# A one-core fp32 attention and MLP kernel: SyncE's order fixed from the first MoE on, probability copies and head loads emitted later

## The chip, the cores and the metric

The kernel runs on one core of a Trainium2 chip. The metric is device time in microseconds (us) of one execution. TensorE (PE) does the matmuls; ScalarE (ACT), VectorE (DVE) and GpSimd (POOL) do the rest of the arithmetic; SyncE (SP) issues nearly all DMA transfers. Each engine works through its own instructions in a fixed order and stands still when the next one has to wait.

## What is computed

```python
def _attn_ref(q, k, v, g_q, g_k):           # q, k, v: (4, 12, 448, 64)
    q_n, k_n = rmsnorm(q, g_q), rmsnorm(k, g_k)
    scores = np.matmul(q_n, k_n.transpose(0, 1, 3, 2)) / np.sqrt(64)
    attn = np.exp(scores - scores.max(-1, keepdims=True))
    attn = attn / (attn.sum(-1, keepdims=True) + 1e-09)
    return np.matmul(attn, v)
# x: attention's output as (1792, 768)
def _moe_ref(x, w_in, w_out):               # 768 -> 2048 -> 768
    r = np.maximum(x @ w_in, 0.0)
    return (r * r) @ w_out
def _moe2_ref(x, w1, w2, w3, w_out):        # 768 -> 1024 -> 1024 -> 768
    return ((x @ w1) * (x @ w2) @ w3) @ w_out
```

The weights of both MLPs come as 64-bit floats, q, k and v as 32-bit ones.

## The kernel before

**Products.** Each fp32 operand is held as a high part and a low part, and each product is three matmuls (high by high, high by low, low by high; `mm3`, lines 411 to 413). In the trace they follow each other at 0.20 us. A unit of weights (128 rows by 384 or 512 columns) feeds nine or twelve matmuls of 448 columns.

**Order of the work.** One loop runs over the 48 heads (B x H, in batch order) and a 49th turn. In a turn, `stage_qk` emits the score matmuls `sc`, `stage_exp` the exponentials into `p`, `stage_t` the transposes of the probabilities of the head before (`pt`, copied to `ptr` and `pte`), `stage_v` their product with v (`kv`), and head norms and transposes of k (`kv` too, copied to `kt`) for later heads. Each head has two halves, s = 0 and s = 1. In between, `fill(n)` emits a stretch of about n matmuls of another generator, six stretches a head; a unit costs 9 or 12 of them. Heads 0 to 11 are filled with `gen_w3o` (w3 by w_out, stored in DRAM as `w3o`, so that the second MLP ends in one product), heads 12 to 23 with `gen_moe(0)`, the MLPs of the first batch, here called the **first MoE**: 16 units of w_in, 12 of w_out, again 16 and 12, then 32 of w1 and w2 and 12 of `w3o`, 100 units in all. Heads 24 to 47 are filled with batches 1 and 2 (the second MoE), and the last batch follows the loop.

**A unit's way.** In the first MoE a 64-bit unit is loaded (line 319, four buffers `raw64`), turned into 32-bit words (ACT line 333, then the low words on ACT line 337 or POOL line 339), joined (DVE line 346, into one of seven buffers `raw`), stored back to DRAM as 32-bit floats for the later batches (line 354, `f_in` and the like), and split into `hl`, the high part on ACT and the low part on POOL or DVE (lines 144 and 150). `advance(u)` emits these ahead of the matmuls of unit u: the low parts up to u + 2 (u + 4 from w1 and w2 on), high parts one further, joins two, words three, loads five further.

**Probabilities.** From head 12 on the probabilities pass through a copy from SBUF to SBUF, `pw` (line 997), which gives them the type that the transposes then read. It is emitted right behind the exponentials that it copies. For odd heads, behind s = 1, four small stores `rsd` (line 1008) send the sums of the exponentials out, and `stage_rows` reads them back as `rsw` in the next turn.

**What sets the order on an engine.** A scheduler orders the instructions of each engine by its own model of the times. `in_order(SP)` marks a point from which `chain()` ties each SyncE instruction to the one emitted before it, so that SyncE issues in emitted order from there on. Before, that point stands at head 24, behind the first MoE. `late` (line 1143) decides whether a turn's loads of the next heads (`load_head`, `load_v`, `load_group`) are emitted at the turn's start or behind its first `stage_exp`; before, it holds from head 25 on.

Of the kernel before, what the change touches and what calls it, by code (L numbers as in the profile page):

```python
# [8 lines left out]
F32 = mybir.dt.float32  # L9
F32R = mybir.dt.float32r  # L10
# [20 lines left out]
def attention_moe_kernel(  # L31
# [15 lines left out]
    nc = tc.nc  # L47
    SP, ACT, DVE, POOL, PE = (e.engine for e in (nc.sync, nc.scalar, nc.vector, nc.gpsimd, nc.tensor))
    B, P, H, C, D = k_nat.shape
    S = P * C  # L50
    QC = q_nat.shape[3]
    MIX = S - 3 * 128
    CHUNKS = (((0, 1), (2, 3)), ((4, 5), (6,)))
    NH = B * H
# [69 lines left out]
    def in_order(*engines):  # L124

        spans.append((nc.cur_bb.bb.instructions[-1], engines))
# [664 lines left out]
    def load_group(g):  # L791
        if not (0 <= g < NH // GH):
            return
        b, h0 = divmod(g * GH, H)
        qk = t1.tile([128, GH * C, D], F32, name="qn", tag="qn")
        qn = qk[:, :GH // 2 * QC]
        kn = t2.tile([P, GH, C, D], F32, name="kn", tag="kn")
        if g == 0:
            nc.sync.dma_start(out=kn[:, 0:2], in_=k_nat[0, :, 0:2])
            load_head(0)  # L800
            nc.sync.dma_start(out=qn[:, :QC], in_=q_nat[0, :, 0])
            load_to(0)
            nc.sync.dma_start(out=kn[:, 2:], in_=k_nat[0, :, 2:GH])
            nc.sync.dma_start(out=qn[:, QC:], in_=q_nat[0, :, 1])
            load_to(1)
        else:
            nc.sync.dma_start(out=kn, in_=k_nat[b, :, h0:h0 + GH])
            nc.sync.dma_start(
                out=qn, in_=q_nat[b, :, h0 // 2:(h0 + GH) // 2].rearrange("p j c d -> p (j c) d")
            )  # L810
        grp[g] = [qk, kn, None, None]
# [161 lines left out]
    def stage_exp(h, s):  # L973
        if not (0 <= h < NH):
            return
        d = heads[h]
        nb, o = d.pop("nb"), d.pop("sc")
        i = h % 2
        if s == 0 and i == 0:
            sums2[h // 2] = small.tile([128, QC], F32, name="sm", tag="sm")  # L980
        sm = sums2[h // 2]
        chunks = CHUNKS[h % 2][s]
        n = len(chunks)
        pp = t3.tile([128, 2, S], F32, name="p", tag="p")
        for j, c in enumerate(chunks):
            p = d["p"][c] = pp[:, j, :]
            if h >= H:
                nc.scalar.activation(
                    out=nb[:, j:j + 1], in_=nb[:, j:j + 1], func=AF.Copy, scale=d["rq"][:, c:c + 1]
                )  # L990
            nc.scalar.activation(  # L991
                out=p, in_=o[j], func=AF.Exp, scale=d["rq"][:, c:c + 1], bias=nb[:, j:j + 1],
                accum_out=sm[:, c:c + 1],
            )
        if h >= H:
            words = t3.tile([128, 2, S], F32R, name="pw", tag="pw")
            nc.sync.dma_start(out=words[:, :n].bitcast(F32), in_=pp[:, :n])
            for j, c in enumerate(chunks):
                d["p"][c] = words[:, j, :]
        if s == 1 and i == 1:  # L1000
            nc.scalar.activation(out=sm, in_=sm, func=AF.Copy, bias=1e-9)
            rs = rss[h // 2 % 2]
            nc.vector.reciprocal(out=rs[:, :QC], in_=sm)
            turned = t2.tile([128, 32], F32, name="rt", tag="rt")
            nc.vector.transpose(out=turned, in_=rs)
            flat = dram.tile([QC, 128], F32, name="rsd", tag="rsd", bufs=2)
            for b in range(0, 128, 32):
                nc.sync.dma_start(out=flat[:, b:b + 32], in_=turned[b:b + QC])
            sums2[h // 2] = flat

    def stage_rows(h):
        if 0 <= h < NH and h % 2:
            flat = sums2[h // 2]
            rows = sums2[h // 2] = t1.tile([128, S], F32, name="rsw", tag="rsw")
            flat = flat.rearrange("c p -> (c p)")
            for r, to, at, n in ((0, 0, 0, S), (D, S - MIX, S, MIX), (D, 0, S + MIX, S - MIX)):
                nc.sync.dma_start(out=rows[r:r + D, to:to + n], in_=flat[at:at + n].partition_broadcast(D))
# [82 lines left out]
    def start_fill(gen, total):  # L1100
        state.update(gen=gen, credit=0.0, left=total)

    def fill(n):
        state["credit"] += n
        while state["gen"] is not None and state["credit"] > 0:
            try:
                k = next(state["gen"])
                state["credit"] -= k
                state["left"] -= k
            except StopIteration:  # L1110
                state["gen"] = None
# [28 lines left out]
    first.close()  # L1140
    for h in range(NH + 1):
        n = W3O / ((H + 1) * 6) if h <= H else (MOE / (H * 6) if h <= 2 * H else (MOE + IN) / (2 * H * 6))
        late = h > 2 * H
        if not late:
            load_head(h + 3)
            load_v(h + 1)
            if h % GH == 0:
                load_group(h // GH + 1)
        stage_qk(h, 0)
        fill(n)  # L1150
        stage_exp(h, 0)
        if h == 0:
            group_prep(0, "rest")
        if late:
            load_head(h + 3)
            load_v(h + 1)
            if h % GH == GH - 1:
                load_group((h + 1) // GH + 1)
        if h % H != 1:
            stage_x(h - 2)  # L1160
        stage_t(h - 1, 0)
        stage_t(h - 1, 1)
        early = H <= h and h % 2 == 0
        fill(n)
        if early:
            stage_k(h + 1)
        stage_lo(h - 1)
        if h < NH:
            v_prep(h)
        fill(n)  # L1170
        stage_rows(h - 1)
        even = H <= h
        if even:
            stage_qk(h, 1)
        if not early:
            stage_k(h + 1)
        stage_t(h - 1, 2)
        stage_t(h - 1, 3)
        fill(n)
        stage_lo(h - 1)  # L1180
        if not even:
            stage_qk(h, 1)
            fill(n)
        stage_exp(h, 1)
        fill(n)
        if even:
            fill(n)
        stage_v(h - 1)
        if h >= 2 * H and h % GH < 2:
            group_prep(h // GH + 1, "qk"[h % GH])  # L1190
        elif h % GH == 1:
            group_prep(h // GH + 1)
        head_prep(h + 2)
        if h and h % H == 0:
            if h != 3 * H:
                fill(1e9)
            stage_x(h - 1)
            if h == H:
                start_fill(gen_moe(0), MOE)
            elif h == 2 * H:  # L1200
                in_order(SP)
                start_fill(gen_late(), MOE + IN)
            elif h == NH:
                start_fill(gen_pair(), MOE)
# [61 lines left out]
```

## Time and profile before

| | |
|---|---|
| runs before | 6176.91, 1163.66 and 1156.78 us, median 1163.66 |
| profiled execution | 1160.01 us, of which the span 1158.2 us |
| mean granted TensorE clock | 0.989 of full speed |
| PE busy | 1124.9 us, 97% of the span |
| DVE busy | 796.4 us, 69% |
| ACT busy | 777.0 us, 67% |
| POOL busy | 605.2 us, 52% |

The profiled execution stands 3.65 us below the median of the runs and 3.23 us above the fastest. The span runs from the first to the last instruction. An engine is busy while one of its instructions runs; on PE, matmuls overlap, and what is not busy is time in which nothing ran there. Waits name the engine that waited, the line of the instruction that waited, and what it waited for. The first MoE takes the stretch from 180 to 450 us.

### The profile page before, as it was taken

To read this page: it belongs to the slowest core of one execution; us is meant where nothing else is said; L and a number is where in the kernel's file an instruction comes from. 1 tells how busy PE (TensorE), PEld (TensorE's weight loads), DVE (VectorE), ACT (ScalarE), POOL (GpSimd) and SP (SyncE) were. 2 spreads that over 40 slices of the span, in tenths; PEclk is the share of its full clock that TensorE was granted. 3 is DMA by queue.
4 is the path that set the end of the run, shared out by engine and by line. 5 is a ranking of instruction groups with operands and counts; after the bars stand their busy time and mean duration, and the time that the engine had idled before them with its cause. 6 is when DMAs were issued, how large, how long until landed. Compare 5 with 4: busy or idle time off the path is not lost. (4 is left out here: it accounts for less than half of the span.)

```text
span 1158.2 us, 18787 instructions
## 1 busy us (share of the span) xinstructions
PE 1124.9 (97%) x5958; PEld 1020.3 (88%) x5958; DVE 796.4 (69%) x1363; ACT 777.0 (67%) x1768; POOL 605.2 (52%) x609
## 2 busy tenths in 40 slices
PE   7889999999999999999999999999999999999998
PEld 4678888988889889989989999999999899999997
DVE  6899888978988754664675755674534315887786
ACT  6889978878978666776766676776754445533352
POOL 3375533544434355956875776684865854021131
PEclk9799999999999999999999999999999999999999
DMA  8767757888888864565655657564546764243423
GB/s 245 255 204 214 234 156 253 300 279 285 298 292 267 282 201 159 166 199 170 224 186 162 203 173 256 177 211 152 188 158 197 223 195 128 68 134 106 128 84 123
DMA packets 130899, 229.74 MB, mean 198 GB/s; under 512 B 17472, under 2 KB 84544, under 8 KB 130800
## 3 DMA queue, kind: packets, MB, share of 16 engines
q1 hardware_dynamic: 129072, 225.79, 61.5%
q10 hardware_dynamic: 1728, 2.75, 0.7%
q8 instruction: 47, 0.77, 0.3%
q14 instruction: 52, 0.43, 0.1%
HBM read 162.53 MB, written 37.05 MB: 172 GB/s over the span
## 5 line engine op out<-in xcount | busy, mean ns | idle before, releaser
L150 POOL TENSOR_TENSOR hl<-raw,hl 128x384 fp32r<-128x384 f32 (+1 forms) x286 | 332.5, 1169 | 286.4 <-ACT hl L144 249.1
L144 ACT ACTIVATE hl<-raw 128x384 fp32r<-128x384 f32 (+1 forms) x405 | 227.3, 567 | 148.9 <-PE mm L413 42.5
L411 PE MATMUL mm<-x,hl 128*128 128x448 f32 (+1 forms) x640 | 238.8, 373 | 1.3 <-ACT x L144 1.3
L412 PE MATMUL mm<-x,hl 128*128 128x448 f32 (+1 forms) x640 | 234.1, 366 | 0.7 <-DVE x L150 0.6
L413 PE MATMUL mm<-x,hl 128*128 128x448 f32 (+1 forms) x640 | 233.7, 365 | 0.0
L411 PE MATMUL mm<-act,hl 128*128 128x448 f32 (+1 forms) x544 | 201.5, 370 | 1.6 <-ACT act L144 1.6
L412 PE MATMUL mm<-act,hl 128*128 128x448 f32 (+1 forms) x544 | 198.6, 365 | 3.1 <-DVE act L150 2.5
L413 PE MATMUL mm<-act,hl 128*128 128x448 f32 (+1 forms) x544 | 197.5, 363 | 0.1
L967 DVE TENSOR_REDUCE nb<-sc 128x1 f32<-128x448 f32 x168 | 102.5, 615 | 69.8 <-PE sc L957 68.6
L411 PEld LDWEIGHTS mm<-x,hl 128*128 128x128 f32 x640 | 121.2, 189 | 11.0 <-ACT x L144 2.6
L412 PEld LDWEIGHTS mm<-x,hl 128*128 128x128 f32 x640 | 121.2, 189 | 10.2 <-DVE x L150 1.6
L413 PEld LDWEIGHTS mm<-x,hl 128*128 128x128 f32 x640 | 121.2, 189 | 9.4
L991 ACT ACTIVATE p<-sc,nb,rr 128x448 f32<-128x448 f32 x168 | 121.5, 725 | 9.6 <-DVE nb L969 6.7
L150 DVE TENSOR_TENSOR ptr<-pt,ptr 128x512 fp32r<-128x512 f32 (+1 forms) x144 | 85.9, 616 | 51.7 <-ACT ptr L144 51.3
L412 PEld LDWEIGHTS mm<-act,hl 128*128 128x128 f32 x544 | 102.5, 188 | 12.2 <-DVE act L150 4.2
L411 PEld LDWEIGHTS mm<-act,hl 128*128 128x128 f32 x544 | 102.7, 189 | 9.3 <-ACT act L144 2.3
L413 PEld LDWEIGHTS mm<-act,hl 128*128 128x128 f32 x544 | 102.6, 189 | 7.9 <-DVE hl L150 0.4
L339 POOL TENSOR_SCALAR raw<-raw 128x384 uint32<-128x384 uint16 (+1 forms) x80 | 54.2, 678 | 95.9 <-DMA raw<-w_out 19.5
L346 DVE SCALAR_TENSOR_TENSOR raw<-raw 128x384 uint32<-128x384 uint32 (+1 forms) x120 | 87.7, 740 | 21.2 <-POOL raw L339 9.4
L333 ACT ACTIVATE raw<-raw 128x384 f32<-128x384 f32 (+1 forms) x120 | 71.6, 603 | 32.9 <-DMA raw<-w 14.5
L956 PE MATMUL sc<-kt,qh 128*128 128x448 f32 (+1 forms) x192 | 75.0, 391 | 14.1 <-ACT kt L144 8.1
L150 DVE TENSOR_TENSOR hl<-raw,hl 128x384 fp32r<-128x384 f32 (+1 forms) x119 | 81.5, 687 | 8.1 <-ACT hl L144 7.9
(153 smaller groups left out, 2127.9 us busy)
## 6 DMA issues: line engine op xcount, KB each, us to landing
pw<-p SPq DMA_DIRECT2D x54, 448.0 KB
raw<-f_in SPq DMA_DIRECT2D x96, 192.0 KB
raw<-f_out SPq DMA_DIRECT2D x72, 256.0 KB
raw<-w_in SPq DMA_DIRECT2D x32, 384.0 KB
raw<-w_out SPq DMA_DIRECT2D x24, 512.0 KB
raw<-w SPq DMA_DIRECT2D x32, 384.0 KB
qt<-q_t SPq DMA_DIRECT2D x48, 224.0 KB
raw<-f SPq DMA_DIRECT2D x56, 192.0 KB
```

The lines of the kernel that those rows point to most:

```text
L144: return nc.scalar.activation(out=out, in_=in_, func=AF.Copy)
L150: return (nc.vector if eng == "v" else nc.gpsimd).tensor_tensor(out=out, in0=in0, in1=in1, op=op)
L333: nc.scalar.activation(out=hi, in_=hi, func=AF.Prelu, scale=2.0**-112, alpha=-(2.0**32))
L339: nc.gpsimd.tensor_scalar(out=t[:, :n, 0], in0=low, scalar1=2.0**-13, scalar2=2.0**-14 - 0.5, op0=ALU.mult, op1=ALU.add)
L346: nc.vector.scalar_tensor_tensor(out=f[:, :n].bitcast(U32), in0=t[:, :n, 1], scalar=3, in1=t[:, :n, 0], op0=ALU.logical_shift_left, op1=AL ...
L411: nc.tensor.matmul(ps, w[:, 0, wk, :], x[0], start=(i == 0), stop=False)
L412: nc.tensor.matmul(ps, w[:, 0, wk, :], x[1], start=False, stop=False)
L413: nc.tensor.matmul(ps, w[:, 1, wk, :], x[0], start=False, stop=(i == last))
L956: nc.tensor.matmul(out, d["qh"][:, at:at + m], d["kt"], start=True, stop=False)
L967: nc.vector.tensor_reduce(out=nb[:, j:j + 1], in_=o[j], axis=AX.X, op=ALU.max, negate=True)
L991: nc.scalar.activation(out=p, in_=o[j], func=AF.Exp, scale=d["rq"][:, c:c + 1], bias=nb[:, j:j + 1], accum_out=sm[:, c:c + 1],)
```

## The change

Three things change, all in what SyncE issues and when.

1. `in_order(SP)` moves from head 24 to head 12: it stands behind the last `fill(1e9)` of `gen_w3o` and ahead of `start_fill(gen_moe(0))`.
2. The copy `pw` leaves `stage_exp` for a function of its own, `stage_words`. For heads 12 to 24 the copy of s = 0 is emitted two stretches behind its exponentials, and that of s = 1 one or two stretches behind. From head 25 on both are emitted directly behind `stage_exp`; for odd heads that puts the copy of s = 1 behind the four `rsd` stores, where it stood ahead of them.
3. `late` holds from head 13 on: the loads of q, k and v for later heads are emitted behind the turn's first `stage_exp`. `load_group` stays where it was for heads up to 24.

```diff
         if h >= H:
-            words = t3.tile([128, 2, S], F32R, name="pw", tag="pw")
-            nc.sync.dma_start(out=words[:, :n].bitcast(F32), in_=pp[:, :n])
-            for j, c in enumerate(chunks):
-                d["p"][c] = words[:, j, :]
+            d["pp"] = pp
...
+    def stage_words(h, s):
+        if not (H <= h < NH):
+            return
+        d = heads[h]
+        chunks = CHUNKS[h % 2][s]
+        n = len(chunks)
+        words = t3.tile([128, 2, S], F32R, name="pw", tag="pw")
+        nc.sync.dma_start(out=words[:, :n].bitcast(F32), in_=d.pop("pp")[:, :n])
+        for j, c in enumerate(chunks):
+            d["p"][c] = words[:, j, :]
...
-        late = h > 2 * H
+        late = h > H
         if not late:
             load_head(h + 3)
             load_v(h + 1)
-            if h % GH == 0:
-                load_group(h // GH + 1)
+        if h <= 2 * H and h % GH == 0:
+            load_group(h // GH + 1)
         stage_qk(h, 0)
         fill(n)
         stage_exp(h, 0)
+        if h > 2 * H:
+            stage_words(h, 0)
...
             load_head(h + 3)
             load_v(h + 1)
-            if h % GH == GH - 1:
+            if h > 2 * H and h % GH == GH - 1:
                 load_group((h + 1) // GH + 1)
...
         fill(n)
+        if h <= 2 * H:
+            stage_words(h, 0)
         stage_rows(h - 1)
...
         stage_exp(h, 1)
+        if h > 2 * H:
+            stage_words(h, 1)
         fill(n)
         if even:
             fill(n)
+        if h <= 2 * H:
+            stage_words(h, 1)
         stage_v(h - 1)
...
             if h == H:
+                in_order(SP)
                 start_fill(gen_moe(0), MOE)
             elif h == 2 * H:
-                in_order(SP)
                 start_fill(gen_late(), MOE + IN)
```

The first place is SyncE's queue where `gen_w3o` ends. Before, these rows stand there; `raw64` from `w_in` are loads of the first MoE's units, `w3o` from `osb` the last stores of `gen_w3o`, and `pw` the copies for head 12.

```order
L826 DMA v_2342<-v_in 128x256
L997 DMA pw_2227<-p_2222 128x896
L439 DMA w3o_99<-osb_2239 128x3x128
L1017 DMA rsw_2267<-rsd_2169 64x448
L1017 DMA rsw_2267<-rsd_2169 64x64
L1017 DMA rsw_2267<-rsd_2169 64x384
L808 DMA qn_4367<-q_nat 128x896
L997 DMA pw_2302<-p_2297 128x896
L439 DMA w3o_99<-osb_2313 128x3x128
L818 DMA qt_2340<-q_t 128x448
L319 DMA raw64_2577<-w_in 128x768
L354 DMA f_in_114<-raw_2540 128x384
```

After the change, these stand at the same last stores.

```order
L1005 DMA rsd_2169<-rt_2167 7x32 x4
L439 DMA w3o_99<-osb_2237 128x3x128
L1025 DMA rsw_2267<-rsd_2169 64x448
L1015 DMA pw_2265<-p_2222 128x896
L1025 DMA rsw_2267<-rsd_2169 64x64
L1025 DMA rsw_2267<-rsd_2169 64x384
L1015 DMA pw_2314<-p_2297 128x896
L439 DMA w3o_99<-osb_2311 128x3x128
L319 DMA raw64_2351<-w_in 128x768
L354 DMA f_in_114<-raw_2155 128x384
L319 DMA raw64_2361<-w_in 128x768
L354 DMA f_in_114<-raw_2356 128x384
```

Of the first MoE's loads from `w_in`, 15 stand ahead of the last `w3o` store before and seven after; `raw64_2351` is the eighth, and the ninth follows right behind it.

The second place is ACT's queue among the units of w1 and w2 of the first MoE, ahead of a copy `kt` that the score matmuls of the next head read. The names in it: line 333 makes the words of a unit, `hl` is the high part of one, `p` are exponentials, `ptr` copies of transposes. Before:

```order
L144 ACTIVATE act_4961<-mm_4874 128x448
L144 ACTIVATE ptr_4710<-pt_4992 128x384
L144 ACTIVATE ptr_4717<-pt_4997 128x384
L144 ACTIVATE hl_5009<-raw_4970 128x384
L333 ACTIVATE raw64_4965<-raw64_4965 128x384
L144 ACTIVATE r_5021<-mm_4964 128x448
L337 ACTIVATE raw64_4965<-raw64_4965 128x384
L144 ACTIVATE hl_5031<-raw_5007 128x384
L333 ACTIVATE raw64_5002<-raw64_5002 128x384
L144 ACTIVATE kt_5045<-kv_5040 128x448
```

After the change, the same copy (now `kt_5043`) stands behind these.

```order
L144 ACTIVATE act_4957<-mm_4872 128x448
L333 ACTIVATE raw64_4720<-raw64_4720 128x384
L144 ACTIVATE vt_4919<-kv_4910 64x448
L144 ACTIVATE vhl_5047<-v_4697 128x4x64
L144 ACTIVATE hl_4858<-raw_4823 128x384
L333 ACTIVATE raw64_4747<-raw64_4747 128x384
L337 ACTIVATE raw64_4747<-raw64_4747 128x384
L144 ACTIVATE r_5019<-mm_4960 128x448
L144 ACTIVATE hl_4880<-raw_4856 128x384
L333 ACTIVATE raw64_4766<-raw64_4766 128x384
L144 ACTIVATE kt_5043<-kv_5038 128x448
```

The `ptr` copies are gone from there, and the words just ahead of the copy belong to older units: before it was the unit of `raw64_5002`, after it is that of `raw64_4766`, which is `raw64_4768` before, six units earlier in the program.

The third place is ACT's queue in the same part of the program, where the high part of one unit (`hl_4775` before, `hl_4773` after) is made for the first matmuls of a product of w1 and w2. Before:

```order
L144 ACTIVATE ptr_4710<-pt_4705 128x512
L144 ACTIVATE ptr_4717<-pt_4712 128x512
L337 ACTIVATE raw64_4654<-raw64_4654 128x384
L144 ACTIVATE hl_4729<-raw_4683 128x384
L333 ACTIVATE raw64_4678<-raw64_4678 128x384
L144 ACTIVATE r_4741<-mm_4677 128x448
L144 ACTIVATE hl_4756<-raw_4727 128x384
L333 ACTIVATE raw64_4722<-raw64_4722 128x384
L144 ACTIVATE hl_4775<-raw_4754 128x384
L333 ACTIVATE raw64_4749<-raw64_4749 128x384
```

After the change:

```order
L144 ACTIVATE hl_4754<-raw_4725 128x384
L991 ACTIVATE p_4981,sm_4980<-sc_4945,nb_4944,rr_3774 128x448
L144 ACTIVATE ptr_4708<-pt_4703 128x512
L144 ACTIVATE ptr_4715<-pt_4710 128x512
L333 ACTIVATE raw64_4650<-raw64_4650 128x384
L337 ACTIVATE raw64_4650<-raw64_4650 128x384
L991 ACTIVATE p_4981,sm_4980<-sc_4949,nb_4944,rr_3774 128x448
L333 ACTIVATE raw64_4674<-raw64_4674 128x384
L144 ACTIVATE hl_4773<-raw_4752 128x384
```

Before, six instructions stand between the two `ptr` copies and that high part, and no exponential is among them. After, five do, one of them an exponential (`p_4981`, of the next head), and the words among them are of units four and five earlier. What else moved is the transposes that the two copies read: in PE's order, 81 rows stand between the last of them and the first matmul of that high part before, and 18 after.

## Rows read from the trace of the kernel before

**Rows 1.** Windows by stage: PE, PEld, DVE, ACT, POOL busy us, clock, DMA share, GB/s
```profile
0.00:180.00 180.00, 161.23 (x865) 136.40 (x866) 155.36 (x315) 148.83 (x340) 83.99 (x108) 0.94 0.71 217
180.00:450.00 270.00, 261.64 (x1396) 237.90 (x1395) 217.35 (x368) 210.08 (x494) 125.38 (x134) 0.99 0.81 269
350.00:415.00 65.00, 62.61 (x332) 56.84 (x331) 52.43 (x91) 50.40 (x122) 28.24 (x31) 0.97 0.82 269
450.00:1158.00 708.00, 702.05 (x3701) 646.01 (x3699) 423.73 (x681) 418.07 (x934) 395.87 (x367) 1.00 0.53 167
```
**Rows 2.** PE's largest wait, 180 to 450: us, times, longest
```profile
PE sc L956 <- ACT kt L144: 5.7, 4, 2.4
```
**Rows 3.** SyncE's largest wait, 180 to 450
```profile
SPq L997 <- ACT ptr L144: 34.0, 8, 5.6
```
**Rows 4.** ACT's largest wait, 350 to 415
```profile
ACT raw L333 <- DMA raw<-w: 9.5, 6, 3.5
```
**Rows 5.** SyncE's timeline: start, duration, line, transfer
```profile
370.19 0.54 SPq L319 DMA_DIRECT2D raw<-w  x1
373.22 1.30 SPq L1008 DMA_DIRECT2D rsd<-rt  x4
...
375.00 0.38 SPq L319 DMA_DIRECT2D raw<-w  x1
...
381.52 0.47 SPq L997 DMA_DIRECT2D pw<-p  x1
```
**Rows 6.** ACT's timeline, same stretch; in brackets the wait ahead
```profile
378.46 0.57 ACT L333 ACTIVATE raw<-raw 128x384 f32<-128x384 f32 x1 [2.54 <-DMA raw<-w]
...
381.30 0.19 ACT L991 ACTIVATION_READ_ACCUMULATOR p<-sc,nb,rr 128x1 f32 x1
...
384.69 0.57 ACT L333 ACTIVATE raw<-raw 128x384 f32<-128x384 f32 x1
385.13 0.55 ACT L144 ACTIVATE kt<-kv 128x448 fp32r<-128x448 f32 x1
```
**Rows 7.** PE's timeline behind the longest wait
```profile
385.74 0.47 PE L956 MATMUL sc<-kt,qh 128*128 128x448 f32 x1 [2.39 <-ACT kt L144]
...
388.57 0.57 PE L413 MATMUL mm<-x,hl 128*128 128x448 f32 x1
388.95 0.57 PE L411 MATMUL mm<-x,hl 128*128 128x448 f32 x1
...
390.06 0.37 PE L412 MATMUL mm<-x,hl 128*128 128x448 f32 x1
390.26 0.37 PE L413 MATMUL mm<-x,hl 128*128 128x448 f32 x1
```
**Rows 8.** Windows with PE idle and a changing clock, columns as in group 1
```profile
30.00:60.00 30.00, 24.96 (x104) 19.74 (x103) 26.81 (x50) 26.19 (x56) 10.51 (x13) 0.81 0.82 269
90.00:120.00 30.00, 28.03 (x166) 24.94 (x165) 29.69 (x55) 27.77 (x62) 18.57 (x23) 1.00 0.78 231
...
386.00:390.00 4.00, 4.00 (x17) 3.37 (x17) 2.55 (x6) 1.08 (x3) 2.18 (x3) 0.57 1.04 327
```
**Rows 9.** Durations of ACT's and POOL's operations, 350 to 415: busy us, mean ns
```profile
L144 ACT ACTIVATE hl<-raw 128x384 fp32r<-128x384 f32 x22 | 11.5, 530 | 0.0
L991 ACT ACTIVATE p<-sc,nb,rr 128x448 f32<-128x448 f32 x10 | 7.2, 720 | 0.1
```
```profile
L150 POOL TENSOR_TENSOR hl<-raw,hl 128x384 fp32r<-128x384 f32 x11 | 12.7, 1155 | 21.2 <-ACT hl L144 20.9
```
**Rows 10.** SyncE's timeline: the last store of w3o
```profile
179.50 0.54 SPq L439 DMA_DIRECT2D w3o<-osb  x1
```
**Rows 11.** SyncE at an odd head of the second MoE; PE reading that copy
```profile
500.50 0.47 SPq L997 DMA_DIRECT2D pw<-p  x1
502.49 1.86 SPq L1008 DMA_DIRECT2D rsd<-rt  x4
```
```profile
508.80 0.63 PE L1030 MATMUL pt<-ident_r,pw 128*128 128x128 f32 x6
```

## Prediction

> **What bounds the kernel now.** I read the windows by stage first. In the profiled execution (1160.0 us, span 1158.2) PE is busy for 261.64 of the 270 us of the first MoE, where nearly all of the change lies, and for 702.05 of the 708 behind it [rows 1]. TensorE paces both, and the change neither adds nor removes a matmul. So what it can win there is what PE stands idle, 8.4 us, and what a lower clock costs. The clock of that stage is 0.99, and the low part of it sits in one place: in the 4 us from 386 to 390 it was granted at 0.57, between the two levels of 1.2 and 2.4 GHz, right behind PE's longest wait, and matmuls there start 0.38 us apart where they otherwise follow at 0.20 [rows 7, 8]. That cost 4 x (1 - 0.57) = 1.7 us. All in all 8.4 + 1.7 = 10.1 us, 0.9% of the time, is the most that an ideal order of this stage would give.
>
> Then PE's waits: of the 8.4 us, 5.7 are four waits of the scores for the copy `kt` on ACT, the longest 2.39 [rows 2, 7]. For the longest I followed the chain back. The `kt` copy starts on ACT at 385.13 and ACT has no gap ahead of it back to 378.46, where it stood 2.54 us for a unit's words [rows 6]. That unit was loaded by SyncE at 375.00, behind the stores `rsd` at 373.22, for which SyncE had stood since it issued the load before, at 370.19 [rows 5]: a transfer on its way for 3.5 us, asked for too late. SyncE stands for 34.0 us of the 270 at line 997 alone, the copies `pw`, because they are in its queue ahead of their exponentials' end [rows 3]: that of 381.52 was issued 0.03 us behind the exponentials' last instruction (381.30 + 0.19) [rows 5, 6]. In the stretch from 350 to 415 ACT's waits for words come to 9.5 us in six [rows 4].
>
> **The change part by part.**
>
> *SyncE in emitted order, copies two stretches late (gain).* A copy emitted two stretches behind its exponentials, some 28 matmuls or 5.7 us, finds them done. So SyncE no longer stands there, and the loads keep their distance of up to four units (the buffers of `raw64`) from their joins. On ACT the words move back too: the order shows them four to eight units later, and those ahead of the `kt` of the longest wait are six units older. A unit's nine matmuls take 9 x 0.20 = 1.8 us, so the word there has 6 x 1.8 = 11 us more for a transfer that was 2.5 us late. I take the four `kt` waits from 5.7 to 1.0 us (-4.7; between nothing, if ACT is late there for another reason, and -5.7), and the slow clock behind the longest of them goes with it (-1.7; between 0 and -1.7). The other waits, 2.7 us, stay.
>
> *The same order, just in time (loss).* What ACT gains ahead of `kt` it pays at the splits. Before, words stand two to ten units ahead of their high parts and these about six units ahead of the matmuls; after, words stand next to their high parts, and these three or four units, among w1 and w2 two to four, ahead of the matmuls. At the third place that the change's section shows, a chain now runs from PE's transposes to PE's matmuls. From the end of the transposes ACT does two `ptr` copies, words, low words, an exponential, words, and the high part. ACT starts copies 0.44 us apart [rows 6], the exponential takes 0.72 + 0.19 with the reading of its sum [rows 6, 9], the high part 0.53 [rows 9]: 5 x 0.44 + 0.91 + 0.53 = 3.6 us, and some 0.3 to see the transposes done. The low part on POOL takes 1.16 [rows 9], so the unit is ready after 5.1 us. PE has, up to the first matmul that needs the low part, 18 matmuls of 0.20 us and eight small transposes of which six took 0.63 [rows 11], 3.6 + 0.8 = 4.4 us. PE would stand 0.7 us, before it nothing. Twelve products of two units each follow among w1 and w2; where no exponentials or `ptr` copies fall into the chain it is 1.8 us shorter and PE doesn't wait. I take half of the twelve: 6 x 0.7 = 4.2, rounded to +4.0. Bounds: 0, since PE's own waits push the chain's start and end alike, and 12 x 1.0 = 12 if every product pays with one further instruction on the way.
>
> *The start of the first MoE (loss).* Before, 15 of the first loads of w_in stand ahead of the last `w3o` store in SyncE's queue, as the first place of the change's section shows; after, the eighth stands behind that store, which was issued at 179.50 [rows 10]. Seven units are there then, 7 x 1.8 = 13 us of matmuls plus the attention's share, and the eighth needs its transfer (3.5 us in the chain above) and words, join and splits, some 3 us: ready at about 187, wanted at about 193. The eight loads that were early are 8 x 0.59 = 4.7 MB, 17 us at the 269 GB/s that the transfers reached in this stage [rows 1], against 16 us of matmuls by then. It nearly fits; I take +1.0, between 0 and +2. The transfers that `gen_w3o` loses could speed that stage up; there PE waits for other engines with a DMA share of 0.71 [rows 1], so I count nothing.
>
> *Loads of the next heads behind the first exponential.* The next heads' q, k and v are used one to three turns later, 22 us each; a delay of one stretch is covered by that. Without that cover it would be a transfer of 3.5 us a head. 0.
>
> *Second MoE.* There only the copies of odd heads' second halves move behind the `rsd` stores: at head 27 from 500.50 to the end of the stores at 502.49 + 1.86 = 504.35, and PE reads the copy at 508.80 [rows 11]. 4.4 us are left for a transfer; I take 0, with 0.4 us for each of twelve such heads, 4.8, as the bound.
>
> Sum: -4.7 - 1.7 + 4.0 + 1.0 = -1.4, so **1160.0 - 1.4 = 1158.6 us**. The profiled execution lies 3.7 below the median of the runs shown, which themselves stand 7 us apart.
>
> **The rivals.**
>
> *All gain.* The chains at the splits and the start are hidden: ACT runs each a little earlier than my count has it, since it waits less for words (9.5 us in six waits from 350 to 415 before [rows 4]). Then 1160.0 - 4.7 - 1.7 = 1153.6. For it: PE has 5.7 of its 8.4 idle us at `kt` [rows 2], and none of its waits in this stage is for a part of the weights. Against it: the hand count above finds the cushion gone.
>
> *Slower: the splits stop PE at each product and the clock falls.* If all twelve products wait 0.8 us, PE loses 9.6. With the 2.4 us that it stands idle in the 65 us from 350 to 415 now, that is 12 of 65, 18%. From 30 to 60 us PE stands idle for 5.0 of 30, 17%, in many small waits, and the clock is 0.81; from 90 to 120 it stands idle for 2.0, 7%, and the clock is 1.00 [rows 8]. At 0.81 the 65 us cost 65 x 0.19 = 12.4 more. Together 1160.0 + 9.6 + 12.4 + 1.0 - 4.7 = 1178.3. It decides from an idle share near that 17%; half of the products paying, as I take, gives (2.4 - 2.4 + 4.0)/65 = 6%, as from 90 to 120, with the clock up. Against it also: of the four `kt` waits only the longest left a low clock behind it that the window shows. The Trainium skill ("TensorE: Matmul & The Clock Gate", section "HAM oscillation — how this bites in real kernels") speaks for this rival: a loop that waits at every tile falls back to the slow clock at every tile, and pays the change of clock each time. The trace agrees with it only in part, by the 0.57 behind a wait of 2.39 us and the 1.00 from 90 to 120 in spite of 7% of waits.
>
> *No effect.* The scheduler had placed loads as well as it could, and the waits go from `pw` to the joins that free `raw64`: the loads then come as late as before, `kt` waits as before, and nothing is paid at the splits: 1160.0.
>
> **How the numbers follow.** Gain and loss about even, as summed: 0.5, with a range of its own from 1153 to 1166 (all of the gain with little loss; 1160.0 - 6.4 + 12 without the clock). All gain: 0.2. Slower: 0.2, spread from 1164 to 1178 and a little beyond with the bound of the second MoE. No effect: 0.1. The range is 1150 to 1173: it leaves out less than 0.05 below and some 0.12 above. Chances go by 2%, 23 us, about what a measurement of this kernel can tell from no change. Faster by that much would need over twice the 10.1 us that the stage has: 0.01. Slower by that much needs the whole slower rival and both other bounds: 0.04. Within: 0.95.
>
> **What would show it.** Right: PE's waits for `kt` from 180 to 450 fall to about 1 us, SyncE's waits at the copies nearly vanish, the clock from 386 to 390 is 1.00, and PE has new waits for `hl` from POOL or ACT among w1 and w2, 0.3 to 1 us each, 4 us in all; at the start up to 2 us of waits for the eighth to sixteenth unit. Wrong: no waits for `hl` (then all gain), a clock under 0.95 from 350 to 415 (then slower), or waits for `pw` in the second MoE.

## The result, and the profile after

The changed kernel takes 1175.05 us (median of six runs, 1173.44 to 1181.04), the kernel before 1158.77 in the six runs by then. The ratio is 1.0148, with an interval from 1.0121 to 1.0174: slower by 1.5%. It leaves out the first run of the kernel before, 6176.91, and is not the quotient of the two medians, which is 1.0140. I had forecast 1158.6, with a range to 1173. The profiled execution of the changed kernel took 1173.72 us, its span 1171.9.

Where the time went is seen best by counting matmuls in the two traces. The 800th matmul, at the end of `gen_w3o`, starts at 168.1 us before and 166.1 after; the 2200th, near the end of the first MoE, at 438.2 and 451.9; the 5800th at 1122.5 and 1136.2. So the stretch from the 800th to the 2200th, called the stage below, took 270.1 us before and 285.8 after, **+15.7 us**; from the 2200th to the 5800th both took 684.3. The 2.0 us gained ahead of the stage tell nothing: two traces of one kernel (free order and free order again, below) differ there by as much, 168.0 and 165.9. All of the loss lies in the first MoE. The windows by stage after, as in [rows 1], show it too: 1311 matmuls from 180 to 450 in place of 1396, and nothing lost behind.

```profile
0.00:180.00 180.00, 163.20 (x878) 138.11 (x879) 153.39 (x312) 145.46 (x334) 79.39 (x103) 0.94 0.61 188
180.00:450.00 270.00, 252.89 (x1311) 221.34 (x1310) 205.17 (x361) 213.38 (x487) 119.30 (x132) 0.99 0.87 278
350.00:415.00 65.00, 60.66 (x307) 50.76 (x306) 53.18 (x99) 53.78 (x129) 25.82 (x32) 1.00 0.90 277
450.00:1158.00 708.00, 705.47 (x3722) 649.20 (x3722) 422.66 (x681) 423.94 (x950) 403.62 (x375) 1.00 0.54 168
```

PE's waits from 180 to 450 after (total, times, longest), which answer to [rows 2]:

```profile
PE pt L1038 <- DVE ptr L150: 8.3, 4, 4.2
PE mm L413 <- POOL hl L150: 2.9, 5, 1.3
PE mm L411 <- ACT hl L144: 2.0, 3, 0.9
...
PE sc L956 <- ACT kt L144: 0.6, 1, 0.6
PE mm L413 <- DVE hl L150: 0.5, 2, 0.3
```

The waits for `kt` have gone from 5.7 to 0.6. In their place PE waits for `ptr`, 8.3 us where it was 1.2 in one wait before, and for parts of the weights, 2.9 + 2.0 + 0.5 = 5.4 us where there were none. Idle time of PE grew by 17.1 - 8.4 = 8.7 us only. The weight loads' queue (PEld), which stands whenever an operand is late, tells the rest: over its whole list of waits in this stretch it stood 11.4 us before and 29.6 after, +18.2. First two of its rows before, then three after:

```profile
PEld sc L956 <- ACT kt L144: 7.2, 4, 2.8
PEld pt L1030 <- DVE ptr L150: 1.6, 2, 1.4
```

```profile
PEld pt L1038 <- DVE ptr L150: 10.1, 8, 4.6
PEld mm L413 <- POOL hl L150: 6.5, 10, 1.7
PEld mm L411 <- ACT hl L144: 3.8, 6, 1.3
```

A matmul is busy for 0.36 us and the next starts 0.20 behind it, so a short interruption hides in the busy time: PE spent 0.193 us of busy time per matmul after (252.89/1311) and 0.187 before. Of the +15.7 us, 8.7 are idle time and 3.0 - 1.7 = 1.3 a lower clock (the windows at the end of this section); the other 5.7 lie in busy time, as such interruptions do.

What stands behind it is on ACT and SyncE. The first row is ACT's largest wait from 180 to 455 after; before it has no such row. The second is SyncE's largest from 180 to 450 after; the third, in a fence of its own, is the same wait before.

```profile
ACT hl L144 <- DVE raw L346: 22.2, 30, 1.9
...
SPq L319 <- DVE raw L346: 89.3, 53, 4.4
```

```profile
SPq L319 <- DVE raw L346: 10.7, 14, 2.3
```

ACT stands thirty times at a high part (line 144) whose unit VectorE has not joined yet. SyncE, freed of its waits at the copies [rows 3], stands at the loads for a `raw64` buffer, which the same joins set free. No load was late for ACT by that: what it waits for loads at line 333 fell from 27.9 us, 180 to 455, to 0.8. The longest of PE's new waits shows how ACT's standing reaches PE. ACT's timeline after, ahead of that wait:

```profile
226.50 0.61 ACT L144 ACTIVATE hl<-raw 128x512 fp32r<-128x512 f32 x1
228.13 0.64 ACT L144 ACTIVATE hl<-raw 128x512 fp32r<-128x512 f32 x1 [1.02 <-DVE raw L346]
228.68 0.66 ACT L333 ACTIVATE raw<-raw 128x512 f32<-128x512 f32 x1
229.23 0.53 ACT L144 ACTIVATE acc<-mm 128x448 f32<-128x448 f32 x1
231.65 0.63 ACT L144 ACTIVATE hl<-raw 128x512 fp32r<-128x512 f32 x1 [1.89 <-DVE raw L346]
...
235.09 1.07 ACT L144 ACTIVATE ptr<-pt 128x512 fp32r<-128x512 f32 x2
```

POOL's, VectorE's and PE's in the same stretch:

```profile
230.24 0.65 POOL L339 TENSOR_SCALAR raw<-raw 128x512 uint32<-128x512 uint16 x1
...
230.93 0.69 DVE L346 SCALAR_TENSOR_TENSOR raw<-raw 128x512 uint32<-128x512 uint32 x1 [2.28 <-POOL raw L339]
...
235.70 1.29 DVE L150 TENSOR_TENSOR ptr<-pt,ptr 128x512 fp32r<-128x512 f32 x2 [0.27 <-ACT ptr L144]
...
236.45 0.75 PE L1038 MATMUL pt<-ident_r,pw 128*128 128x128 f32 x4 [4.24 <-DVE ptr L150]
```

The words of a unit start on ACT at 228.68; POOL makes the low words at 230.24, VectorE joins at 230.93, and ACT, whose next instructions are the high part and what stands behind it, has stood from 229.76 to 231.65. POOL came to the low words no sooner because a low part stood ahead of them, from 228.85 to 230.15. Counted over the thirty waits, the join was held up three ways: in 16 (11.1 us) the words were done and the join began as VectorE ended other work; in four (5.1 us) the low words stood behind other work on POOL; in ten (5.9 us) ACT's own words ended last.

The transposes of 230.27 wait in PSUM for their `ptr` copies, which stand behind those high parts and start at 235.09; the next transposes need the space, and PE stands 4.24 us. Only a part of that is ACT's standing: of the 4.4 us between the transposes' end at 230.72 and 235.09, ACT stands 0.9 for the join and works nearly all of the rest through the seven instructions ahead of the copies. With that wait the clock falls, as it did with the longest wait before [rows 8]: 0.50 from 236 to 242, while the place of before, 386 to 390, is at 1.00.

```profile
386.00:390.00 4.00, 3.85 (x19) 3.16 (x18) 3.86 (x7) 3.13 (x8) 1.57 (x2) 1.00 0.87 281
...
236.00:242.00 6.00, 5.55 (x20) 4.91 (x21) 4.59 (x9) 3.68 (x9) 2.99 (x4) 0.50 0.84 283
```

### The profile page after: what moved, and what is told of

The parts are those of the page before. It is cut to its first block, busy times and chain, and to the rows that moved or that the text cites. A ratio compares the mean times of both kernels' runs of the same rounds, so it can differ in the third digit from the quotient of the medians.

```text
span 1171.9 us, 18787 instructions
## 1 busy us (share of the span) xinstructions
PE 1132.0 (97%) x5958; PEld 1017.9 (87%) x5958; DVE 787.7 (67%) x1363; ACT 782.8 (67%) x1768; POOL 602.3 (51%) x609
## 5 line engine op out<-in xcount | busy, mean ns | idle before, releaser
L150 POOL TENSOR_TENSOR hl<-raw,hl 128x384 fp32r<-128x384 f32 (+1 forms) x286 | 329.2, 1158 | 343.2 <-ACT hl L144 276.5
L411 PEld LDWEIGHTS mm<-x,hl 128*128 128x128 f32 x640 | 120.5, 188 | 13.7 <-ACT hl L144 3.5
L346 DVE SCALAR_TENSOR_TENSOR raw<-raw 128x384 uint32<-128x384 uint32 (+1 forms) x120 | 83.2, 695 | 30.0 <-POOL raw L339 12.6
L150 DVE TENSOR_TENSOR hl<-raw,hl 128x384 fp32r<-128x384 f32 (+1 forms) x119 | 78.3, 660 | 14.0 <-ACT hl L144 12.6
L144 ACT ACTIVATE ptr<-pt 128x512 fp32r<-128x512 f32 (+1 forms) x144 | 73.4, 541 | 11.2 <-PE pt L1038 11.2
L487 DVE TENSOR_TENSOR gf<-mm,r 128x448 f32<-128x448 f32 x48 | 29.8, 622 | 72.5 <-ACT r L483 70.8
```

The costliest lines, as they stand in the source:

```text
L144: return nc.scalar.activation(out=out, in_=in_, func=AF.Copy)
L150: return (nc.vector if eng == "v" else nc.gpsimd).tensor_tensor(out=out, in0=in0, in1=in1, op=op)
L346: nc.vector.scalar_tensor_tensor(out=f[:, :n].bitcast(U32), in0=t[:, :n, 1], scalar=3, in1=t[:, :n, 0], op0=ALU.logical_shift_left, op1=AL ...
L411: nc.tensor.matmul(ps, w[:, 0, wk, :], x[0], start=(i == 0), stop=False)
L487: nc.vector.tensor_tensor(out=gf, in0=ps, in1=r, op=ALU.mult)
```

## The experiments

Four theories were tried. A: SyncE's emitted order from head 12 costs, because it places the words of a unit next to their high part in ACT's queue. B: the copies two stretches later cost. C: the later loads of the next heads cost. D: SyncE's order costs by itself, whatever ACT's queue looks like. "Lead" below is how many further units' words have started on ACT when a unit's high part starts, counted in each trace and averaged over twenty units; the second, third and fourth twenty of the first MoE are given. The stage is that from the 800th to the 2200th matmul.

| kernel | ratio to before | 95% interval | stage, us | lead | ACT's waits for joins, us |
|---|---|---|---|---|---|
| before | 1 | | 270.1 | 4.0, 2.8, 2.6 | no row |
| changed | 1.0148 | 1.0121 to 1.0174 | 285.8 | 0.2, 0.1, 0.2 | 22.2 |
| order alone | 1.0112 | 1.0056 to 1.0167 | 283.8 | 0.2, 0.2, 0.2 | 26.8 |
| free order | 0.9966 | 0.9939 to 0.9994 | 264.3 | 4.0, 3.0, 2.9 | no row |
| near copies | 1.0117 | 1.0061 to 1.0173 | 282.0 | 0.4, 0.2, 0.1 | 24.0 |
| early loads | 1.0169 | 1.0120 to 1.0218 | 286.0 | 0.2, 0.1, 0.3 | 19.0 |
| ahead by 2 | 1.0210 | 1.0182 to 1.0238 | 284.1 | 0.8, 0.1, 0.2 | 20.6 |
| ahead by 4 | 1.0045 | 1.0025 to 1.0066 | 269.9 | 3.4, 1.9, 1.1 | 5.4 |
| units free | 1.0014 | 0.9996 to 1.0032 | 269.9 | 3.9, 2.2, 1.6 | 0.7 |
| free, ahead by 2 | 1.0063 | 1.0038 to 1.0088 | 271.4 | 4.9, 4.0, 3.8 | no row |
| ACT tied | 1.0097 | 1.0072 to 1.0122 | 281.3 | 0.0, 0.0, 0.0 | 31.9 |
| ahead by 4, first MoE only | 1.0078 | 1.0049 to 1.0107 | 276.7 | 2.5, 1.0, 0.7 | 14.3 |
| late loads alone | 0.9981 | 0.9961 to 1.0001 | 266.9 | 4.0, 2.8, 2.8 | no row |
| free order again | 0.9954 | 0.9930 to 0.9978 | 263.9 | 4.0, 3.0, 3.0 | no row |

**One part at a time.** The kernel before with the order alone:

```diff
             if h == H:
+                in_order(SP)
                 start_fill(gen_moe(0), MOE)
             elif h == 2 * H:
-                in_order(SP)
```

> The kernel before with one edit: SyncE issues in emitted order from head 12 on; copies and loads of the next heads are emitted where they were. Theory A (the early emitted order is the cause: SyncE's loads no longer run ahead of it, so the words of a unit stand next to its high part in ACT's queue, ACT stands there for the join on VectorE, and the high parts and ptr copies behind come late for PE): ratio to before 1.012 to 1.025, since SyncE now also stands at each copy in order; ACT waits for joins at the hl splits 15 us or more between 180 and 460 (before: none among its larger waits). Theory B (the copies of the probabilities two stretches later are the cause) and theory C (the later loads of the next heads): ratio 0.997 to 1.003.

Measured 1.0112, a little under A's range and far above the other one, the stage 13.7 us longer than before. The changed kernel with that part undone, free order:

```diff
             if h == H:
-                in_order(SP)
                 start_fill(gen_moe(0), MOE)
             elif h == 2 * H:
+                in_order(SP)
```

> The changed kernel with one edit undone: SyncE's emitted order begins at head 24 again, so that the scheduler orders SyncE through the first MoE; the copies stay two stretches late and the loads late. Theory A: ratio to before 0.997 to 1.003, ACT's waits for joins at hl under 5 us, PE's waits for ptr as before (about 1 us from 180 to 450). Theories B and C: 1.012 to 1.018, with PE's waits at the transposes still 8 us or more.

Measured 0.9966, at the lower end of A's range, faster than before, with the stage 5.8 us shorter. All that PE waited for in the first MoE, 180 to 455, more than 0.1 us:

```profile
PE sc L956 <- ACT kt L144: 2.7, 3, 1.5
PE pt L1038 <- DMA pw<-p: 2.4, 2, 1.5
```

The waits at `ptr` are gone although the copies are as late as in the changed kernel, so B falls. The next two undo the other parts, near copies (`stage_words` directly behind `stage_exp` for all heads) and early loads:

```diff
-        late = h > H
+        late = h > 2 * H
```

> The changed kernel with the copies emitted directly behind their exponentials for all heads; emitted order from head 12 and late loads stay. Theory A: ratio 1.012 to 1.025, as the changed kernel or slower, because SyncE stands at the copies. Theory B: below 1.005, PE's waits at the transposes for ptr back to about 1 us. Theory C: 1.012 to 1.018.

> The changed kernel with the loads of the next heads at the turn's start through the first MoE, as before; emitted order from head 12 and late copies stay. Theories A and B: ratio 1.010 to 1.020. Theory C: 0.997 to 1.004.

Measured 1.0117, again a little under A's range, and 1.0169: neither takes the loss away. B and C are out. Whether near copies help a little under the emitted order (1.0117 against 1.0148) the intervals don't tell.

**Is it SyncE's order, or ACT's?** The next three keep SyncE's emitted order and give the words their lead back in two ways. First by emitting further ahead:

```diff
-    JOIN_AHEAD = 2
-    WORD_AHEAD = 3
+    JOIN_AHEAD = 4
+    WORD_AHEAD = 5
...
-    LOAD64_AHEAD = 5
+    LOAD64_AHEAD = 7
```

> The changed kernel with the units' loads, words and joins emitted two units further ahead (joins 4, words 5, loads 7 units ahead of the low part in place of 2, 3 and 5); SyncE in emitted order from head 12. In ACT's order the words of the first half of the first MoE then stand 1 to 3 units ahead of their high parts, those of the second half still next to them. Theory A (words next to high parts make ACT stand for the joins): ratio to before 1.005 to 1.013, ACT's waits for joins at hl between 8 and 20 us from 180 to 455 (changed kernel 22). Theory D (SyncE's order costs by itself, by transfers that start late and by transposes that come later, whatever lead the words have): 1.012 to 1.018, as the changed kernel.

Measured 1.0210, a miss for A by its ratio, and above D's range too. Two things came together. The numbers hold for `gen_w3o` as well, which I had not thought of, and there the kernel lost 11 us (800th matmul at 177.1 against 166.1). And in the first MoE the lead hardly grew (0.8, 0.1, 0.2), and the stage hardly shrank, 284.1 against 285.8. With 6, 8 and 10:

> As the run before, with joins 6, words 8 and loads 10 units ahead. In ACT's order the words stand 2 to 6 units ahead of their high parts, except among the last units. Theory A: ratio 0.997 to 1.006, ACT's waits for joins at hl under 8 us. Theory D: 1.010 or more.

Measured 1.0045. With leads of 3.4, 1.9 and 1.1 ACT's waits for joins fall to 5.4 us and the stage takes 269.9, as before the change. The second way takes the units' loads and stores out of the emitted order and leaves the rest in it:

```diff
-            nc.sync.dma_start(out=t[:, :n, :], in_=src...)
+            untied.add(nc.sync.dma_start(out=t[:, :n, :], in_=src...).ins.name)
...
-            nc.sync.dma_start(out=dst, in_=raws[i][:, :dst.shape[-1]])
+            untied.add(nc.sync.dma_start(out=dst, in_=raws[i][:, :dst.shape[-1]]).ins.name)
...
-                mine = [i for i in traced[:starts[m + 1]] if i.engine == e]
+                mine = [i for i in traced[:starts[m + 1]] if i.engine == e and i.name not in untied]
```

> The changed kernel with the loads of the 64-bit units and the stores of their 32-bit words taken out of SyncE's emitted order; the copies, the rsd and rsw transfers and the loads of the next heads stay in it from head 12. Words then stand 2 to 4 units ahead of their high parts as in the free order. Theory A: ratio 0.995 to 1.003, ACT's waits for joins under 5 us. Theory D: 1.010 or more.

Measured 1.0014, the stage 269.9 us, leads of 3.9, 2.2 and 1.6. So it is the units' loads and stores, tied between the other transfers, that cost most: 15.9 of the 21.5 us of stage that the changed kernel has over the free order (285.8 and 264.3). The copies, `rsd`, `rsw` and the heads' loads in emitted order are not free of cost: with the same late copies and late loads the free order has 0.9966 and a stage 5.6 us shorter. That much is left for D, or for the somewhat shorter lead (2.2 and 1.6 where the free order has 3.0 and 2.9). PE's waits from 180 to 455 (lines are one higher here):

```profile
PE pt L1039 <- DMA pw<-p: 4.5, 4, 2.1
PE sc L957 <- ACT kt L145: 4.0, 3, 1.9
```

Deeper emission in the free order:

> The kernel with SyncE free through the first MoE, late copies and late loads (which took 0.9966 of the time before), with joins 4, words 5 and loads 7 units ahead. Words gain about one unit of lead. Theory A: there are next to no waits for joins left to win, so 0.993 to 1.000; a gain would have to come from PE's last waits for kt and the copies, 5 us. Theory D expects the same.

Measured 1.0063, above what either theory gave. Its 800th matmul starts at 172.4, 4.4 us later than in the first trace of the kernel that it was made from, so here too part of the loss is in `gen_w3o`; the stage is 7.1 us longer than there, with no waits for joins but 6.0 us of PE's waits for the copies `pw`, 2.4 there. A lead over what the free order had brings nothing more; why the rest was lost is not explained.

The reverse leaves SyncE free and ties ACT's words. For that the words are also emitted two units nearer, the joins and stores one:

```diff
-        nc.scalar.activation(out=hi, in_=hi, func=AF.Prelu, ...)
+        word = nc.scalar.activation(out=hi, in_=hi, func=AF.Prelu, ...).ins
+        if U0 + 8 <= i < U1:
+            tc.add_manual_dep(word, last["hi"], why, reason="word behind the high part before")
...
+            less = 1 if U0 <= i < U1 - 12 else 0
...
-            upto("word", i + WORD_AHEAD, lambda k: is64(k) and words(k))
-            upto("join", i + JOIN_AHEAD, lambda k: is64(k) and join(k))
+            upto("word", i + WORD_AHEAD - 2 * less, lambda k: is64(k) and words(k))
+            upto("join", i + JOIN_AHEAD - less, lambda k: is64(k) and join(k))
```

> The kernel of the second run (SyncE free through the first MoE, late copies, late loads, 0.9966 of the time before) with one thing forced on ACT: in the first MoE the words of a unit (line 333) may start only behind the high part of the unit before, so that words stand right ahead of their high parts, as they do in the changed kernel, while SyncE stays free to issue loads early. The words and joins are emitted one and two units nearer for that. Theory A (ACT's order is what costs): ratio 1.008 to 1.020, ACT's waits for joins at hl 15 us or more from 180 to 455, PE waits for hl and ptr. Theory D (SyncE's order costs by itself): 0.995 to 1.003, PE's waits as in the second run.

Measured 1.0097 where the same kernel without these edits had 0.9966, the stage 281.3 us in place of 264.3. ACT's largest wait and PE's, 180 to 455 (VectorE's line 349 is line 346 of the others):

```profile
ACT hl L144 <- DVE raw L349: 31.9, 39, 1.9
...
PE pt L1042 <- DVE ptr L150: 13.2, 7, 2.9
```

SyncE, though free, then stands for joins as in the changed kernel:

```profile
SPq L319 <- DVE raw L349: 90.3, 59, 3.8
```

So words held next to their high parts on ACT, with SyncE left free, are enough to bring most of the loss, 17.0 us of stage, with ACT's waits and SyncE's long waits for buffers; D falls as the main cause. How much the nearer emission does without the tie was not run. One thing came out otherwise than expected: PE does not wait for `hl` here, but for `ptr` and, 4.0 us, for the copies `pw`. Last, the deeper emission held to the first MoE, with 6, 7 and 9:

```diff
             i = pos["lo"]
+            more = 4 if U0 <= i < U1 - 12 else 0
...
-            upto("join", i + JOIN_AHEAD, lambda k: is64(k) and join(k))
+            upto("join", i + JOIN_AHEAD + more, lambda k: is64(k) and join(k))
```

> The changed kernel with joins 6, words 7 and loads 9 units ahead of the low part, for the units of the first MoE alone; gen_w3o keeps 2, 3 and 5. The fifth and sixth run changed these numbers for gen_w3o too, and lost 9 and 3 us there; in the first MoE the one was 14 us and the other 0.3 us behind the kernel before. Theory A: 0.996 to 1.003 with ACT's waits for joins at hl under 9 us. Theory D: 1.010 or more.

Measured 1.0078, between the ranges of A and D, with the waits for joins above the 9 us expected. Words and loads stand one unit nearer here than with 8 and 10, and that unit counts: leads of 2.5, 1.0 and 0.7, waits for joins of 14.3 us, the stage 276.7. By stage, the kernels with the emitted order rank by lead: 0.1 to 0.8 units with 282 to 286 us, 0.7 to 2.5 with 276.7, 1.1 to 3.4 and 1.6 to 3.9 with 269.9. Of the 8.0 us between the medians, 6.6 are in the stage. The profiled execution lost 4.4 us more in the last matmuls (last section).

**What the lead does not account for.** PE's waits for `ptr` do not go away with a longer lead. Ahead by 4, with ACT's waits for joins down to 5.4 us, from 180 to 455:

```profile
PE pt L1038 <- DVE ptr L150: 6.9, 6, 2.4
PE kv L1084 <- ACT ptr L144: 2.5, 2, 2.0
PE kv L1084 <- DVE ptr L150: 0.2, 1, 0.2
```

That is 9.6 us for these copies, as in the changed kernel with `pte` counted in (9.4 in the stage). What the longer lead took away are the waits for the weights' parts, 5.4 us to none, and the low clock. Another order moved too, that of PE: the section on the change counted 81 rows between two transposes and the matmuls that followed at one place, and 18 after. Counted through the stage, two successive groups of transposes stand at most ten matmuls apart 17 times in the changed kernel, 19 times ahead by 4, 13 times with ACT tied, and 13 to 22 times in every kernel of the table where PE waits over 5 us for `ptr`; in the six others 2 to 5 times. So the waits for `ptr` go with where PE's transposes stand, at least as much as with ACT's standing. No run holds PE's order, so the shares stay open.

**What made the free order faster.**

> The kernel before with one edit: through the first MoE the loads of the next heads are emitted behind a head's first exponentials (late from head 13 on); SyncE free, copies where they were. It splits the gain of the second run: if the late loads make it, 0.994 to 0.998; if the late copies make it, 0.999 to 1.003.

> The kernel of the second run again, in five rounds, beside the others: 0.994 to 0.999 if its gain of 0.3% stands.

Late loads alone gave 0.9981, with an interval that reaches 1.0001; the free order again 0.9954 (0.9930 to 0.9978). Some of the gain may come from each part; the runs don't separate them. The free order, that is the change without its first part, beats both kernels: 1151.58 us beside 1158.18 for the kernel before.

## Why the prediction was wrong

- **SyncE no longer stands at the copies: right.** Its largest wait at the line of the copies in the first MoE is 1.2 us, 34.0 before [rows 3]. But its time went to the loads, at the joins that free `raw64`, 89.3 us in place of 10.7. I had that move among the rivals ("no effect") and concluded that loads would come late for ACT as before; they did not (0.8 us of waits, 27.9 before): it was the joins that came late.
- **Gain at `kt`: right.** 5.7 to 0.6 us, -5.1 where I took -4.7, and the clock at 386 to 390 is back at 1.00. The free order also brought it to 2.7 and 2.1 us, without the emitted order.
- **The step that failed: "the other waits, 2.7 us, stay", beside a price of "just in time" that had ACT only work.** I had read from the order that words now stand next to their high parts, and priced that by adding up the durations of ACT and POOL. What such a place also costs is ACT standing at the high part until the join is there, up to 1.9 us at a time, thirty times, 22.2 us in all, and whatever is queued behind it late. The weights' parts were mis-sized little: 5.4 us of waits on PE against +4.0. Among w1 and w2, where I had put them, they are 3.9 us (350 to 415), in part by luck, since ACT stood 4.5 us for joins in that stretch and the sum has none of it. (Its 0.3 us for seeing the transposes done had no row, and its 0.44 us is the pitch of 128x384 copies, where the two `ptr` copies of 128x512 take 1.07 together.) What I put at nothing were PE's waits for `ptr`: 1.2 us became 8.3, the longest 4.24 with 6 x (1 - 0.50) = 3.0 us of slow clock at its end. That the transposes had moved closer stood in the section on the change; I made a chain of it for one high part, and not for the transposes that follow. I had looked for trouble among w1 and w2 alone; in this trace the largest loss, 8.2 us between the 1000th and the 1200th matmul (37.2 us before, 45.5 after), lies at the units of w_out, around 220 to 245 us. How the `ptr` waits divide between ACT's standing and PE's own order is open.
- **A second error, in the measure.** I set the stage's 8.4 us of PE idle time, with the slow clock, as the most that waits cost, and counted losses the same way. Each short wait also costs what the overlap of matmuls hides: +8.7 us of idle time stand beside +15.7 us of stage. The weight loads' waits, +18.2, are nearer to it.
- **The start: not seen.** The eighth load was issued at 177.34, right behind the last `w3o` store as the order had it, but from the 800th to the 1000th matmul it took 36.9 us before and 36.4 after, where I took +1.0. The 0.59 MB of that term count a unit's load and its store; the load alone is 0.39.
- **Second MoE: right, nothing.** At head 27 the copy now goes out at 518.57, behind the stores, and PE's only wait from 455 to 880 is for `kt`:

```profile
176.70 0.60 SPq L439 DMA_DIRECT2D w3o<-osb  x1
177.34 1.42 SPq L319 DMA_DIRECT2D raw<-w_in  x1
...
516.43 1.82 SPq L1005 DMA_DIRECT2D rsd<-rt  x4
518.57 0.47 SPq L1015 DMA_DIRECT2D pw<-p  x1
```

```profile
PE sc L956 <- ACT kt L144: 1.5, 1, 1.5
```

- **The rivals.** The slower one gave nearly the measured time (1178.3) by a mechanism that did not occur where it was placed: from 350 to 415 PE stands idle 4.34 of 65 us, 7%, and the clock is 1.00, as its own condition said. Its 0.2, and the 0.12 left above 1173, were too little for a change whose order showed every unit's cushion gone.
- One line of the section on the kernel is wrong: the low parts run up to u + 4 from the start of the first MoE on, not from w1 and w2 on. No term rested on it.

Why a tie on SyncE moves ACT's instructions is seen in the leads of the table: the order of all engines is made together, and where the units' loads are tied between other transfers (order alone, near copies, early loads), the words' lead is gone in the queue of ACT as it is laid down, and it comes back where the loads and stores are untied. What in the scheduler's model does this, and why PE's transposes then stand closer, stays open.

## What to carry to other kernels

An order forced on one queue is read by what it does to the other engines' queues: find where a step now stands close behind the step that it needs on another engine, and charge the engine that waits there not only its own durations but also the other engines' work in between, and then each instruction queued behind it. Do the same for each buffer that is refilled sooner than before, here that of the transposes. A lookahead that was bought by letting transfers run free is lost when they are tied to the pace of others; tie only those whose order matters (units free took away 15.9 us of the loss), or leave the queue free, which was fastest here. Read interruptions of a pipelined engine from the time between two counted matmuls or from its weight loads' waits, not from its idle time alone.

## What the runs showed of the hardware

At the end of PE's wait of 4.24 us the granted clock is 0.50 from 236 to 242, longer than behind the wait of 2.39 us before. The 0.57 there is a mean over 4 us with full clock at its edges, not a level between the two: from 387 to 389 it is 0.50 as well, 1.2 GHz of 2.4. After the change, from 350 to 415, with 7% idle in waits of up to 1.30 us, the clock stays at 1.00. The length of a wait alone doesn't tell: in ahead by 4 a wait of 2.39 us left the clock at 1.00, as one of 2.99 us ending at 228.09 did with ACT tied.

```profile
285.59 0.53 PE L1038 MATMUL pt<-ident_r,pw 128*128 128x128 f32 x4 [2.39 <-DVE ptr L150]
...
286.00:290.00 4.00, 3.81 (x22) 3.17 (x21) 3.29 (x7) 2.39 (x5) 2.53 (x3) 1.00 0.91 333
```

I had not expected a further difference: in three profiles (order alone, ahead by 2, ahead by 4 in the first MoE only) the matmuls from the 5000th to the 5800th start 0.2067 us apart, in the others 0.2027, with a granted clock of 1.00 in both. Windows from 1040 to 1100, before and then ahead by 4 in the first MoE only:

```profile
1040.00:1100.00 60.00, 60.00 (x297) 55.60 (x297) 46.08 (x77) 21.07 (x41) 9.49 (x9) 1.00 0.40 116
```

```profile
1040.00:1100.00 60.00, 60.00 (x292) 54.49 (x292) 44.00 (x78) 19.95 (x39) 9.86 (x9) 1.00 0.38 112
```

Over 800 matmuls that is 3.2 us. Up to the 4600th matmul the three go at the pace of the others, so the stage is not touched. The cause stays open. It seems to belong to the execution and not to the kernel: in all three the profiled execution is the longest of the four, by 2.8 to 7.7 us, and the others have no trace.
